# A new written-out order for the same 2,997 steps: DeltaNet attention and an MLP block

## The chip, the cores and the metric

The kernel runs on one core of a Trainium2 chip. The metric is the time of one execution on the device, in microseconds (us). TensorE is called PE here, VectorE DVE, ScalarE ACT, GpSimd POOL and the queue of SyncE SP.

## What is computed

Everything is fp32. The reference runs a DeltaNet recurrence over q, k, v of shape (4, 8, 768, 48), that is 4 batches, 8 heads, 768 tokens, head size 48:

```
state = 0                                       # per batch and head, 48 x 48
for t in range(768):
    kt = k[t] / (norm(k[t]) + 1e-6)
    y[t]  = q[t] @ state
    state = state + beta[t] * outer(kt, v[t] - state^T kt)
```

The heads are then laid side by side (x has 384 columns), and an MLP with a layer norm follows:

```
xn  = (x - mean(x)) / sqrt(var(x) + 1e-6) * g_ln
out = x + relu(xn @ w_ch1) @ w_ch2              # 384 -> 1536 -> 384
```

## The kernel before

The 768 tokens are cut into 12 chunks of 64. For a chunk the recurrence becomes matrix products plus the inverse of a unit lower triangular 64x64 matrix for each of the 32 (batch, head) pairs.

- **Start, chunk 0.** `first_inverse` builds that inverse by doubling, in five levels n = 1..5, for two groups g of heads. A level is a product E_n (PE, L722), a copy of E_n under a mask (DVE, L731), a product Z_n (PE, L741), transposes back (DVE, L687) and copies into the inverse `xt` (ACT, L681). Ahead of it stand the transposed keys (`first_kt`, PE L568, ACT L573), the products of keys with keys (`first_g`, PE L635), the key sums and norms (`first_norms`, ACT L594, DVE L595 to L602) and the first scaled G: `gsb <- product * ndb`, DVE L695. The masks are made on DVE from two iotas of POOL: six masks, each of three steps "ma" (L395), "mb" (L402) and "mask" (L408). POOL also copies an identity into seven buffers (L421).
- **Chunks 1 to 11.** `rows_inverse` solves 32 rows for two chunks at a time on DVE (62 small multiply and subtract steps, L860 and L867), `join` (PE L898 and L904, with a DVE transpose L888 ahead) doubles 32 to 64, and `recur` carries the state (PE L983, L1017, L1024, L1034). Results go through DRAM between these stages: `gd` (G), `xd` and `xt` (the inverse), `xld` and `xnt` (normed rows).
- **MLP.** Chunk 0 is done by halves (L1326, L1341). Chunks 1 to 3 multiply by w_ch1 directly (L1300), later chunks with a scheme of fifteen products (`fifteen`, L1221, with DVE L1241); the second product uses a scheme of seven (`seven`, L1423, with sums and differences of `h_all` on POOL, L1410, and outputs on DVE, L1441).

Nothing of this runs in the order in which the code states it. `add()` only notes a step with its engine and what it reads and writes; a step is one instruction of DVE, ACT, POOL or SP, or one group of matmuls on PE. A string `ORDER` then lists all 2,997 step numbers, and `emit()` issues them in that order:

```
for n in stated_order():
    if n < 0:
        self.filler()
        continue
    fn, deps = self.steps[n]
    assert deps <= out and n not in out
    fn()
```

Each engine works through its own steps strictly in the order of the list, waiting where an operand is not ready. DMA starts are steps of the queue that issues them: most are SP's, the loads of weights are ACT's, some loads of keys and beta POOL's. The entry `z` in the list issues the filler, a matmul of an identity with a broadcast column (128x128 by 256 columns, two passes, L1515), whose result nobody reads.

The steps that the prediction speaks of by number: 12 `eye`; 14, 17, 20, 23, 26, 29 the "ma" steps of masks 0 to 5; 82 and 89 the key sums; 110 the first scaled G; 122 and 124 E_1 of the two groups; 126 and 132 Z_1; 355 the first `u` product (L1000); 200 Z_5 of group 1; 359 the first half of the output of chunk 0 (L1024); 339 G of chunk 2 (L775); 577 the DVE transpose ahead of `join(3)`; 578 its first product; 941 a product of L1423.

Of the kernel before, what the change touches and what calls it, by code (L numbers as in the profile page):

```python
# [59 lines left out]
1 9 49 50 8 63 52 51 10 5 250 54 71 11 56 0 6 14 7 12 47 62 53 48 23 13 72 55 36 18 64 42 26 37 61 27 58 60 77 81 15 28 17 32 331 43 73 88 29 40 65 79  # L60
24 19 82 68 78 21 89 74 95 16 76 20 90 75 98 83 80 84 22 85 34 91 86 96 87 33 25 92 97 93 4 35 30 94 110 99 100 111 101 112 114 66 116 122 113 211 210
117 102 70 208 123 115 103 118 233 126 104 124 69 127 105 107 128 119 31 121 106 125 120 252 129 223 132 38 221 138 108 134 39 139 109 222 251 140 135
204 131 130 234 136 3 674 144 137 67 57 133 213 254 146 224 141 149 2 209 413 235 44 142 147 45 253 244 212 143 256 145 150 255 242 205 41 154 153 416
155 243 148 238 151 236 332 152 225 675 156 z 215 157 240 159 158 214 237 239 160 216 162 161 257 46 241 168 164 166 333 206 165 334 245 207 417 163
419 169 174 170 343 258 226 175 172 259 173 415 171 176 381 177 425 260 227 261 167 178 344 217 228 180 179 248 414 263 345 335 386 346 219 182 262
677 186 264 181 420 183 265 266 192 267 268 189 246 336 269 270 218 193 229 220 188 185 184 187 59 271 196 422 190 272 191 231 273 426 194 274 197 199
275 198 421 338 276 247 355 382 277 195 249 384 356 337 359 278 678 279 679 280 200 230 281 361 232 363 387 339 282 364 201 383 391 283 202 203 385
389 373 357 284 375 388 376 374 396 285 590 390 340 358 341 588 591 286 681 342 401 379 287 392 288 289 594 394 290 953 291 347 589 595 292 348 380
293 360 393 350 598 294 362 395 592 368 599 349 442 295 680 441 406 296 351 427 369 815 593 444 297 814 428 443 298 676 602 424 299 352 687 596 300
603 353 301 445 302 399 303 304 377 597 612 305 817 306 606 354 307 418 308 613 607 309 365 423 600 310 397 311 614 689 312 601 366 313 610 314 816  # L70
315 615 611 316 409 604 317 819 318 319 616 818 605 320 404 321 617 322:324 407 608 398 483 325 378 400 402 326 367 629 487 609 370 481 403 371 618
630 480 429 372 446 627 486 485 619 682 628 405 482 633 484 631 329 634 408 330 447 632 410 327 328 448 449 956 479 821 635 820 411 637 809 620 810
638 488 636 621 489:491 641 492 494 622 639 430 493 691 623 495 640 690 496 642 431 497 686 498 624 499 500 822 643 435 434 693 645 501 433 962 502
688 432 503 644 651 957 1100 504 505 436 692 506 507 652 438 508 439 509 647 440 510 437 811 653 511 512 964 450 666 1102 513 654 514 1099 451 515 655
516 517 454 518 965 519 966 1104 520 656 961 455 521 951 456 452 522 463 958 457 646 458 657 453 1215 464 649 465 807 523 459 658 808 524 466 460 1105
525 659 963 467 461 1106 694 950 468 683 462 955 526 660 1112 527 684 1101 528 469 1111 529 473 648 650 695 530 475 474 531 470 476 532 471 661 472
696 533 857 534 1114 535 697 536 967 855 537 858 1213 538 539 685 662 540 856 541 823 542:545 825 546:548 861 663 549:551 863 552 862 553:556 667 867
557 864 968 668 665 869 824 879 868 702 880 959 664 960 859 1214 669 873 860 560 1272 559 672 1103 865 561 812 670 558 705 826 477 866 699 874 698 870
701 888 969 412 706 871 703 885 700 875 704 671 872 1216 566 881 889 625 876 877 895 563 1217 813 567 878 1222 890 564 569 915 882 570 827 562 891 568
886 898 571 565 916 707 1107 896 626 899 572 1115 1212 900 708 883 576 892 709 574 884 901 573 1224 710 1116 893 575 902 954 887 894 917 903 1380 1113  # L80
828 904 1221 1558 711 713 905 829 923 918 577 712 897 924 832 714 715 673 925 716 833 717 906 718 834 926 719 912 835 907 841 836 927 1274 842 919 928
837 1560 908 838 929 920 843 913 839 909 844 941 840 720 910 721 830 845 921 914 846 847 722 922 1377 851 723 578 1264 1223 849 930 724 1557 1226 579
942 725 580 1562 831 931 1218 852 943 850 1118 853 932 848 726 581 1117 933 854 727 582 944 911 728 934 945 729 935 730 970 936 1227 731 938 1376 583
732 937 971 1225 972 585 1273 1228 584 587 1210 1563 733 946 734 1006 952 735 939 736 737 1004 738 974 973 947 1005 739 1007 586 1028 1010 740 1029
1119 1564 1559 975 1229 1011 1031 1008 1561 741 1385 742 1570 940 743 1569 1012 744 1009 745 746 1016 747 1013 976 748 749 1014 1387 750 1017 1572
1386 751 478 1211 979 752 1571 1015 1378 753 754 977 980 755 981 756 1018 1389 757 988 982 989 1384 1573 978 990 1379 1020 983 758:760 1022 761 1021
762 991 984 763 1390 1019 764 1108 985 765 949 1023 1034 1391 766 1230 986 767 948 1109 768 769 1388 1037 770 987 771 1110 1026 772 773 992 774 775
993 994 1038 776 1027 1024 995 1670 1044 1231 996 1030 1120 1265 1025 1275 1047 1035 1121 1039 1064 1040 1048 1122 1045 780 1041 1032 777 1049 1033
778 1065 1042 1036 779 1050 1043 1066 1126 1046 1051 1000 1054 1219 1266 1233 998 1268 997 1232 1276 999 1267 1127 1052 1055 1131 1053 1067 1565 1128
1061 1056 1072 1124 1270 1068 1125 1073 1392 1220 1069 1129 1074 1002 1057 1130 1001 1070 1075 785 1003 784 1058 1269 1076 781 1234 1079 1277 782 1059  # L90
1080 1271 783 1060 1077 1081 1680 2035 1078 786 1373 1062 1090 787 1123 1082 790 1091 789 1083 788 1063 1278 1092 2037 1279 1084 1682 1132 1071 1093
1681 1085 791 1302 1133 1086 1280 793 1134 792 1135 794 1136 1138 795 1094 1284 1137 2039 1139 1140 1235 1141 1285 1142 1281 1143 796 1305 1095 1303
1236 1668 1290 2034 1096 1684 1144 1087 1374 1145 2041 1282 1146 1291 1673 2036 1147 1148 1574 1088 1149 1237 1150 1283 1669 1151 1152 1239 1098 1153
1154 797 1155 1156 1296 1157 799 800 1158 1241 1686 1159 1288 1576 1160 1297 1304 1248 1161 2040 1311 1162 1289 1286 1238 1249 1250 1163 1381 1294
1164 1858 1287 1382 1165 1240 1383 1679 801 1312 1675 1295 1292 1251 1089 1166 1167 1685 1313 1168 1293 1674 1393 1252 1242 1169 798 1253 1855 1308
1243 1395 1375 1309 1244 1857 1306 1245 802 1318 1397 1097 1314 1300 1394 1319 1307 1298 1170 1575 1301 1171 803 805 1172 1246 1321 1173 1315 1247
1174 1322 1299 1255 1316 804 1310 806 1323 1254 1317 1396 1175 1256 1320 1683 1176 2038 1398 1672 1177 1178 1324 1179 1399 1338 1180 1325 1676 1181
1339 1326 1340 1327 1328 1182 1341 1260 1346 1183 1342 1184 1257 1347 1185 1343 1186 1259 1348 1344 1329 1687 1258 1349 1335 1353 1330 1350 1187 1354
1863 1188 1331 1189 1853 1351 1190 1402 1336 1191 1263 1345 1352 1261 1400 1262 1192 1404 1193 1194 1355 1865 1411 1195 1332 1412 1196 1356 1197 1413
1364 1198 1333 1414 1365 1334 1337 1450 1199 1441 1366 1200 1401 1440 1451 1455 1201 1427 1403 2150 1577 1357 1405 1430 1406 1367 1851 1358 1457 1439  # L100
1566 1852 1415 1431 1456 1359 1416 1429 1407 1688 1443 1408 1859 1567 1432 1409 1418 1368 1444 1202 1452 1410 1435 1203 1369 1433 1204 1454 1458 1370
1205 2047 1453 1417 1208 1460 1434 1459 1419 1361 1862 1464 1442 1461 1568 1436 1462 1866 1466 1437 1671 1467 1463 1867 1438 1578 1465 1360 1445 1690
1362 1446 1469 1468 1579 1447 1689 1422 1428 1471 1448 1470 1449 1474 2049 1472 1477 1581 1584 1475 1473 1580 1480 1860 1423 1861 1478 1363 1483 1479
1481 1583 1476 1691 1421 1484 2051 1489 1420 1694 1486 1485 1582 1693 1490 1692 1487 1502 1496 1588 1491 1503 1587 1488 1677 1492 1678 1504 1695 1585
1493 1206 1505 1494 1586 1506 1497 1495 1371 1701 1426 1516 1869 1589 1498 1696 1703 1868 1507 1499 1699 1529 1207 1424 2042 1509 1697 1517 1372 1744
# [1547 lines left out]
```

## Time and profile before

| | |
|---|---|
| time, median of 3 runs | 510.0 us (508.62 to 510.16) |
| the profiled execution | 510.58 us, of which its span is 508.8 us |
| mean granted PE clock | 0.965 |
| PE busy | 488.6 us (96%), 9606 matmul passes |
| DVE busy | 353.8 us (70%) |
| ACT busy | 249.0 us (49%) |
| POOL busy | 275.6 us (54%) |
| chain that ended last | PE 90%, DVE 5%, issue 2%, POOL 1%, DMA 1% |

A busy time is a sum over the instructions of an engine. The clock is the share of full speed that PE was granted. In the chain that ended last every step is followed back to what released it, so 90% of PE says that over most of the span the end waits for PE alone.

### The profile page before, as it was taken

The page shows a single profiled execution, that of the slowest core. Times are in us where ns is not written, and L with a number is a line of the kernel's source. Part 1 is how long each engine was busy: PE and PEld are TensorE (multiplying, and loading weights), DVE is VectorE, ACT ScalarE, POOL GpSimd, SP SyncE. Part 2 cuts the span into 40 slices and gives each one's busy share as a digit, 9 for nine tenths or more (in the row PEclk, how much of TensorE's full clock was granted, in tenths as well). Part 3 has the DMA queues.
Part 4 walks back from the last instruction along what each step waited for, and adds up shares of the span by engine and source line. Part 5 has one row for each costly group of instructions (what it writes and reads, how often), then busy time and mean ns, then how long its engine had stood idle before and what let it go on. Part 6 is the DMA issues. An engine that isn't in the chain of part 4 may idle for free.

```text
span 508.8 us, 22190 instructions
## 1 busy us (share of the span) xinstructions
PE 488.6 (96%) x9606; PEld 447.6 (88%) x9606; DVE 353.8 (70%) x780; ACT 249.0 (49%) x620; POOL 275.6 (54%) x430
## 2 busy tenths in 40 slices
PE   7778999999899999999999999999999999999996
PEld 3667988788788898899999999999999999999996
DVE  9668987997679648896649898568899328143251
ACT  5758873643544524627435535435563257363230
POOL 5464537264755496438894363492543850645633
PEclk9756799999999999999999999999999999999999
DMA  8988796667656566546834434766154402211101
GB/s 168 293 160 190 249 200 85 98 152 130 90 86 87 187 119 119 65 99 149 194 58 62 94 62 135 150 94 97 50 92 106 111 20 45 60 48 46 24 18 31
DMA packets 196097, 54.99 MB, mean 108 GB/s; under 512 B 186076, under 2 KB 189404, under 8 KB 196000
## 3 DMA queue, kind: packets, MB, share of 16 engines
q1 hardware_dynamic: 189920, 40.58, 41.9%
q10 hardware_dynamic: 3872, 9.83, 6.0%
q0 software_dynamic: 2208, 3.17, 3.8%
q8 instruction: 75, 1.23, 1.0%
q14 instruction: 22, 0.18, 0.1%
HBM read 36.64 MB, written 16.91 MB: 105 GB/s over the span
## 4 chain that ended last, share of the span: by engine, by line
PE 90%; DVE 5%; issue 2%; POOL 1%; DMA 1%; SPq 0%; ACT 0%; DVEq 0%; POOLq 0%; ACTq 0%
PE f L1423 29%; PE f L1221 22%; PE f L1300 9%; PE f L1326 4%; PE f L1341 3%; PE by L983 2%; PE by L1024 2%; PE two L983 2%; PE by L775 2%; PE two L1017 2%; PE two L775 2%; PE two L1034 2%; PE f L775 1%; DMA xt<-xd 1%; PE by L741 1%
## 5 line engine op out<-in xcount | busy, mean ns | idle before, releaser
L1410 POOL TENSOR_TENSOR h_all<-h_all 128x256 f32<-128x256 f32 x123 | 89.9, 742 | 135.1 <-PE f L1423 121.3
L1423 PE MATMUL f<-w_sb,h_all 128*128 128x192 f32 x492 | 109.8, 332 | 1.6 <-DVE rstd L967 1.6
L1423 PEld LDWEIGHTS f<-w_sb,h_all 128*128 128x128 f32 x492 | 81.8, 190 | 3.6 <-issue 1.9
L1423 PE MATMUL f<-words,h_all 128*128 128x192 f32 x396 | 84.5, 330 | 0.3 <-POOL h_all L1410 0.3
L860 DVE TENSOR_TENSOR tmp<-xb,gb 128x87 f32<-128x87 f32 (+21 forms) x186 | 73.7, 396 | 4.9
L867 DVE TENSOR_TENSOR xb<-xb,tmp 128x87 f32<-128x87 f32 (+21 forms) x186 | 73.6, 396 | 4.8
L1241 DVE TENSOR_TENSOR h_all<-h_all,f 128x512 f32<-128x512 f32 x96 | 63.5, 682 | 14.3 <-PE f L1221 13.2
L1423 PEld LDWEIGHTS f<-words,h_all 128*128 128x128 f32 x396 | 66.6, 190 | 1.7 <-POOL h_all L1410 1.0
L1300 PE MATMUL f<-xnt,w_sb 128*128 128x256 f32 x216 | 50.2, 382 | 0.0
L349 POOL DMA_DIRECT2D tb<-in_k_dram x64 | 42.0, 660 | 10.3 <-DVE kt L755 9.4
L1243 ACT ACTIVATE h_all<-h_all 128x512 f32<-128x512 f32 x48 | 28.5, 624 | 34.6 <-DVE h_all L1241 34.3
L1300 PEld LDWEIGHTS f<-xnt,w_sb 128*128 128x128 f32 x216 | 40.2, 190 | 5.3
L1237 ACT COPY h_all<-f 128x512 f32<-128x512 f32 x48 | 26.2, 590 | 34.3 <-PE f L1221 17.4
L1441 DVE TENSOR_TENSOR o<-f,x 128x192 f32<-128x192 f32 x33 | 11.6, 352 | 38.9 <-PE f L1423 22.3
L1221 PE MATMUL f<-words,w_sb 128*128 128x128 f32 x256 | 31.7, 276 | 0.0
L1309 ACT ACTIVATE h_all<-f 128x256 f32<-128x256 f32 x36 | 13.3, 382 | 35.1 <-PE f L1300 34.9
L1221 PEld LDWEIGHTS f<-words,w_sb 128*128 128x128 f32 x256 | 30.0, 192 | 0.2
L1221 PE MATMUL f<-xnt,w_sb 128*128 128x128 f32 x192 | 25.4, 276 | 0.0
L542 POOL TENSOR_TENSOR w_sb<-words 128x768 uint32<-128x768 uint32 (+1 forms) x11 | 15.0, 1365 | 17.7 <-DVE words L529 13.3
L1221 PEld LDWEIGHTS f<-xnt,w_sb 128*128 128x128 f32 x192 | 23.7, 192 | 0.1
L1326 PEld LDWEIGHTS f<-xnt,w_sb 128*128 128x128 f32 x144 | 19.2, 200 | 3.3 <-issue 0.2
L1088 ACT ACTIVATE xnt<-xnt,g_sb 128x256 f32<-128x256 f32 x27 | 12.5, 498 | 19.2 <-DMA xnt<-xld 19.1
(246 smaller groups left out, 958.4 us busy)
## 6 DMA issues: line engine op xcount, KB each, us to landing
words<-in_moe_w_ch_dram ACTq DMA_DIRECT2D x10, 768.0 KB, 5.2
gd<-gsb SPq DMA_DIRECT2D x11, 512.0 KB, 3.6
v<-in_v_dram SPq DMA_DIRECT2D x24, 192.0 KB, 4.3
kr<-in_k_dram SPq DMA_DIRECT2D x46, 96.0 KB, 3.6
out_dram<-o SPq DMA_DIRECT2D x44, 96.0 KB, 2.8
xld<-xlt SPq DMA_DIRECT2D x9, 384.0 KB, 3.3
xnt<-xld SPq DMA_DIRECT2D x36, 96.0 KB, 3.2
gb<-gd SPq DMA_DIRECT2D x44, 64.0 KB, 3.0
```

The source lines that it names most:

```text
L349: add(eng, cost, lambda: QUEUE[eng].dma_start(out=out_, in_=in_), r, w, bulk=n * ns / 16e3, **kw)
L775: nc.tensor.matmul(pair[hp][half(e ^ (hp & n)), (g * NP + j) * C : (g * NP + j + 1) * C], kt[drows(hp), l], rt[drows(hp), i],)
L860: lambda j=j, n=n, w=w, t=t: nc.vector.tensor_tensor(out=t, in0=xv[:, 0:n, j : j + 1].to_broadcast([np_, n, w]), in1=gv[:, j : j + 1, j + ...
L867: "DVE", dve(n * w), lambda t=t, rest=rest: nc.vector.tensor_tensor(out=rest, in0=rest, in1=t, op=ALU.subtract),
L1221: nc.tensor.matmul(wide(p[:, 128 * n : 128 * n + 128]), w[n // 2][:, n % 2 * 128 : n % 2 * 128 + 128], r, start=start and n == 0, stop=Tru ...
L1237: add("ACT", act(512), lambda: nc.scalar.copy(o, p), pk, ok)
L1241: add("DVE", dve(512), lambda: nc.vector.tensor_tensor(out=o, in0=o, in1=p, op=op), pk, ok)
L1243: add("ACT", act(512), lambda: nc.scalar.activation(o, o, ACTF.Relu), [], ok)
L1300: nc.tensor.matmul(p[:, 0:TOK], w1_sb[:, t, f * 128 : (f + 1) * 128], xnt[:, t], start=(t == 0), stop=(t == KC - 1))
L1326: nc.tensor.matmul(p[:, 0:128], w1_sb[:, t, f * 128 : (f + 1) * 128], xnt[:, t, cols], start=(t == 0), stop=(t == KC - 1))
L1410: add(eng, cost, lambda: e.tensor_tensor(out=out_, in0=x, in1=y, op=op), r, w, port=2 if eng == "Pool" else 1, pr=-2)
L1423: lambda f=f, t=start and f == 0: nc.tensor.matmul(p[:, 0:D2], lhs(f), rhs[:, f], start=t, stop=(f == F2 - 1), skip_group_check=True),
```

## The change

Only the string `ORDER` changes; all its 93 lines are new. The set of step numbers is the same, every step still comes after those that it depends on, and `z` occurs three times instead of once. The first lines of the diff, cut:

```
 ORDER = """
-1 9 49 50 8 63 52 51 10 5 250 54 71 11 56 0 6 14 7 12 47 62 53 48 23 13 72 55 36 18 64 42 26 37 61 27 58 60 77 81 15 28 17 32 331 43 73 88 29 40 65 79
-24 19 82 68 78 21 89 74 95 16 76 20 90 75 98 83 80 84 22 85 34 91 86 96 87 33 25 92 97 93 4 35 30 94 110 99 100 111 101 112 114 66 116 122 113 211 210
...
+62 5 52 49 47 71 50 63 51 48 8 54 9 6 10 1 7 53 0 57 11 72 56 251 55 12 4 60 14 32 42 61 250 74 76 331 77 81 40 88 78 65 82 34 73 58 79 64 41 83 68 95
+17 36 89 33 97 13 37 90 80 98 29 30 15 3 84 75 100 96 23 85 31 86 91 99 16 87 27 110 210 35 101 18 66 111 102 92 112 113 115 93 103 94 122 26 28 70 19
...
```

Read engine by engine, it does this:

| engine | before | after |
|---|---|---|
| DVE, ahead of step 110 | 38 steps: all "ma" and "mb", masks 0 to 4, the norms of both groups | 28 steps: only masks 0 and 5 are made, the norms of group 1 (92 to 94) follow later |
| DVE, between 110 and the copy of E_1 of group 1 (125) | 9 steps, among them mask 5 | 20 steps, among them masks 1 to 4 |
| POOL, first steps | iotas, beta, a 0.97 us memset, identity matrix, then copies | two loads of beta, iotas, identity matrix, another load of beta, then memsets and copies mixed |
| PE, first level | 122, 102, 126, 124, 107, 106, 132, 138 | 102, 122, 126, 106, 107, 124, 138, 132, z |
| PE, fourth level | 177 (E_4 of group 1), 180 (Z_4 of group 0), 335, 186, 192 | 180, 177, 186, 335, 192 |
| PE, the filler | once, ahead of E_3 of group 1 | once ahead of step 204 (a product of queries and keys), once between 355 and 200, once between 359 and 339 |
| PE, after 355 | 359, 200, 339 | z, 200, 359, z, 339 |
| DVE, near `join(3)` | 577 ahead of the sums 929 and 921 and of 839 and 845 (layer norm of chunk 2) | 577 behind them |
| SP | transfers spread between each other in one way | 386 transfers in another order; two thirds of them change their place |

Of PE's 816 steps 501 keep their order among each other (the longest common subsequence), of DVE's 780 steps 565, of ACT's 589 steps 317, of POOL's 426 steps 206, of SP's 386 steps 127.

## The prediction

> **What bounds it now.** Read first: the busy table and the 40 slices on the page.
>
> ```profile
> span 508.8 us, 22190 instructions
> PE 488.6 (96%) x9606; PEld 447.6 (88%) x9606; DVE 353.8 (70%) x780; ACT 249.0 (49%) x620; POOL 275.6 (54%) x430
> PE   7778999999899999999999999999999999999996
> PEclk9756799999999999999999999999999999999999
> ```
>
> PE is full in all slices (12.7 us each) but the first four and the last, and its clock is below full only in the first five. The chain that ended last agrees: 90% PE, 5% DVE, 2% issue. So a new order can gain in three places only: PE's idle time, its clock, the passes it is given. Its idle time, from the waits of PE and PE's timeline:
>
> ```profile
> PE f L775 <- issue: 2.5, 2, 1.6
> PE f L1423 <- DVE rstd L967: 1.6, 1, 1.6
> PE by L741 <- issue: 1.5, 1, 1.5
> ```
>
> Columns: who waits for whom, us in total, times, longest. PE idles 15.9 us ahead of its end at 504.6; 13.0 of them lie before 50 us, and 2.9 after, of which 1.60 is one gap at 138.25 and 0.81 a stall at 143.02. The "issue" stalls lie where PE's count of weight loads and matmuls reaches 449, 705, 961, 1217, exactly 256 apart, and queue q8 (instruction) has 75 packets of 16 KB: code is being fetched. They hang on the count, which a new order keeps (each filler adds four).
>
> The clock, from the windows view, columns as named in its head: PE, PEld, DVE, ACT and POOL busy, granted clock, DMA share, GB/s:
>
> ```profile
> 18.90:22.31 3.41, 3.41 (x65) 3.08 (x68) 1.21 (x4) 2.46 (x5) 2.95 (x4) 0.50 0.99 391
> 46.20:49.62 3.42, 2.70 (x76) 2.44 (x72) 3.21 (x9) 3.30 (x7) 2.17 (x3) 0.50 0.90 85
> 49.62:53.03 3.41, 3.41 (x107) 3.22 (x99) 3.34 (x8) 3.10 (x8) 1.91 (x3) 0.50 0.54 96
> 53.03:56.44 3.41, 3.38 (x43) 2.96 (x42) 3.41 (x5) 2.31 (x7) 2.55 (x3) 0.50 0.77 246
> 56.44:59.86 3.42, 3.42 (x91) 3.08 (x93) 3.18 (x9) 2.80 (x6) 0.53 (x1) 1.00 1.03 404
> ```
>
> The clock changes on a grid of 3.41 us; from 15.48 it is half to 56.44, apart from 22.31 to 25.72 and 42.79 to 46.20, and full from there on. Each full stretch followed a half one that was busy for 3.38 or 3.41 and held 1.1 to 2.0 us of 128x128 passes (by the same view of one line: L568 1.97 in 18.90 to 22.31 and 1.11 in 39.38 to 42.79, L1326 1.98 in 53.03 to 56.44). One condition alone was not enough: 49.62 to 53.03 was busy throughout, but with 64-row products, and half clock followed; 29.14 to 32.55 held the filler (1.22) but was busy for 3.05 only, and half clock followed.
>
> **The change, part by part.** All sums are made against the profiled execution, 510.58 us (508.8 span and 1.8 around it). The median, 510.0, lies 0.58 below it; about 0.3% (1.5 us) is what a measurement of this kernel can tell from no change.
>
> *a. The start, to step 355 (begins 46.37).* Up to 110 (begins 11.14) DVE is the bound, and the timeline shows why it is late:
>
> ```profile
> 4.19 0.62 POOL L421 COPY gsb<-u 128x512 f32<-128x512 f32 x1
> 4.74 0.62 POOL L421 COPY pt<-u 128x512 f32<-128x512 f32 x1
> 5.30 0.61 POOL L421 COPY gsb<-u 128x512 f32<-128x512 f32 x1
> 3.80 2.38 DVE L402 TENSOR_SCALAR xb<-xb 128x64 int32<-128x64 int32 x1
> 6.09 1.06 DVE L402 TENSOR_SCALAR xb<-u 128x64 int32<-128x64 int32 x1
> 8.10 0.54 DVE L595 TENSOR_REDUCE ksum<-xln 128x8 f32<-128x384 f32 x1
> ```
>
> Start, duration, instruction. An L402 step takes 0.18 undisturbed; this one took 2.38, until three copies of POOL back to back were over, the next 1.06 beside two more. Key sum 82 had its operand from ACT at 6.63 and ran at 8.10. The new order takes 10 steps net from ahead of 110 (mask steps of 0.18 to 0.22, starts some 0.1 apart: 1.1 us) and may let 82 run near 6.7. Against it: POOL issues two loads of beta (0.72 and 0.52) ahead of the iotas that all masks start from, so these come 1.2 later; its copies now follow load 57, two memsets of 0.97 between them, and so start near 4.9 and last past 8.5; and the steps open to starvation (14, 17, 29, 30, 15, all TENSOR_SCALARs) now stand before and between the two key sums, so that a stall of 1.06 to 2.38 is passed on to 110. Without any stall 110 comes 0.9 earlier (sums at 6.7 and 7.6, then the seven small steps to 110 as before); with one stall of 1.06 to 2.38 it comes 0.2 to 1.5 later. I take +0.8, since copies back to back did this both times they met an L402. [...]
>
> From 110 on the five levels are one chain of PE, DVE and ACT. Each edit there: E_1 of group 0 before L568's last passes, the masks between 110 and 125 (nine steps more, of about 0.1 to 0.2 at their starts; cover: DVE waits for PE in this stretch, 1.2 busy of 3.41 in the window at 18.90), and the filler ahead of 204: at nothing, the 1.60 code stall at 22.97 hides them (the price without it 1.15 for the filler). The filler ahead of E_3 of group 1 goes: -1.15 (row L1515 at 30.98), but the code stall behind it (34.67, 1.53) begins later in count and takes back about half: -0.5. Z_4 of group 0 ahead of E_4 of group 1: nothing to +0.4, since PE waits 0.99 at 37.70 for DVE's copies and the swap asks for the other one first; I take +0.35, as that wait is the nearest row. DVE's transposes 187 and 188 ahead of copy 193: +0.35. With 0.8 from above: 0.8 - 0.5 + 0.35 + 0.35 = **+1.0** at step 355, bounds -0.7 (no starvation) and +1.6 (a second one).
>
> *b. The fillers behind 355 and 359.* Two of 1.15 at half clock are 2.30; PE idled 0.65 at 48.02, waiting for the DVE copy ahead of 359, and step 200 now stands there too: 2.30 - 0.65 = **+1.65**; at full clock half of it less the same gap, +0.5. Nothing else covers them: PE has no other idle time from 48.67 to 63.
>
> *c. The clock.* The fillers are 128x128 passes, and with 355 ending near 49 they start at about 49 and 52: at least one, 1.15 us, lies in 49.62 to 53.03, which was busy already. By the pattern above that window is followed by full clock: from 53.03 instead of 56.44. 3.41 us at half clock are 1.7 of full work: **-1.7**; one window earlier it would be -3.4, no change 0. I take the middle value: the window that ends at 49.62 gets a part of one filler at most. [...]
>
> *d. The steady state.* The gap at 138.25:
>
> ```profile
> 135.79 0.71 DVE L888 STREAM_TRANSPOSE xnj<-xt 128x512 f32<-128x512 f32 x1 [2.63 <-DMA xt<-xd]
> 139.35 0.35 DVE L1441 TENSOR_TENSOR o<-f,x 128x192 f32<-128x192 f32 x1
> ```
>
> DVE's queue is in order: 577 waited 2.63 for a transfer of 5.08 us, and the sums behind it (929, 921), which free the PSUM that L1423 wants, came late. Now they stand ahead of 577, and those behind 577 have no such hurry: -1.6. Elsewhere room moves both ways. I counted PE's work between the last issue of the transfers and the first product of each of eleven joins: six have more or the same, five less; the least of these are e4, from 9.2 to 6.6 us, and e6, from 10.0 to 6.3. Their need is the 5.08 of the row plus 0.71 for the transpose, 5.8, so they still fit by 0.5 to 0.8. SP now reaches 20 transfers (before: 5) less than 3 us after one that they depend on, 3 us being the page's usual landing; each can hold SP's later issues. I allow +0.4, bounds 0 and +4. Sum **-1.2**. The tail is in nearly the same order: 0.
>
> **Sum.** +1.0 + 1.65 - 1.7 - 1.2 = -0.25, so 510.3 on the profiled execution, **509.7** against the median. The range of this case alone: 508.6 to 511.4.
>
> **Rivals.**
> 1. *Full clock by 49.62.* The window from 46.20 grows dense (its 0.72 of idle filled by a filler) and the rate doubles at once: c is -3.4, fillers +1.65: sum -1.95, **508.0**. For it: that 1.11 of wide passes was enough at 39.38; against it: with 355 later, less than one filler fits there. [...] Chance .22.
> 2. *A fast start.* POOL's copies miss the L402s or yield: a is -0.7, sum -1.95, **508.1**. Against it: both stalls of 2.38 and 1.06. Chance .11.
> 3. *Paid fillers without the clock* (the other side). 355 begins 1.6 later, so the fillers straddle 49.62 and neither window holds enough; half clock to 56.44: +1.6 + 1.65 + 0 - 1.2 = +2.05, **512.0**. It decides if no full-rate window begins before 56.4. For it: the dense window at 49.62 and the filler at 30.98, which brought nothing. Chance .22.
> 4. *SP held back* (slower too). A transfer waited for in SP's queue delays those of e4 or e6 by over 0.8 us, the point from which PE waits; two or three gaps like that at 138.25 (1.6 each): d is +2 instead of -1.2, sum +2.95, **513**. For it: 20 against 5 tight starts. Against it: after 50 us PE waited for a transfer, through DVE, only at 138.25. Chance .15.
> The change not doing what it says is the same as a's middle value: masks moved, but starvation takes the room.
>
> **How the numbers follow.** The forecast has .30, and its range lies within 1.5 us of 510. Rivals 1 and 2 (.33) make "faster", 3 and 4 (.37) "slower". The likeliest time is 509.7. Down, the range takes in both fast rivals at once (-0.7 + 1.65 - 3.4 - 1.2 = -3.65, 506.4, put at 506.5); up, rival 4 with 0.5 more, 513.5.
>
> **What would show it.** Right: 110 later than 11.14 and an L402 of over 1 us near POOL's copies; 355 near 47.4; granted clock 1.00 from 53.0; the wait of L1423 for rstd L967 gone; PE's end near 504.3. Wrong: 110 before 10.5; full clock at another place; PE waits of over 0.5 us after 60 us on L898 or L1423, behind a DMA; a code stall off the counts named.

## The result and the profile after

| | before | after |
|---|---|---|
| median of 21 executions each, in turn on the same chips | 508.19 us (506.35 to 511.52) | 510.53 us (509.08 to 516.78) |
| ratio, 95% interval | 1 | 1.0048 (1.0028 to 1.0067) |
| mean over more executions (standard error) | 508.46 us (0.12), the 148 that stand beside the experiments | 510.35 us (0.28), 20 of these 21 and 12 later ones |
| the profiled execution, its span | 510.58, 508.8 us | 510.01, 508.1 us |

The new order is slower by 0.48% over the first 21 executions and by 1.9 us (0.37%) over all. One execution of after, at 516.78, was in a slower state and is left out of the ratio and of the mean. Executions of one and the same program differ by 0.6 to 2.0 us (standard deviation over its executions), and the profiled execution of before was a late one: 2.1 us above the mean of its kernel. The profiled execution of after lies 0.3 below the mean of its own. So the two spans, 508.8 and 508.1, tell the wrong way round, and no single pair of profiles shows where 1.9 us went. What follows rests on events that come again in several traces, and on means over executions.

The page after, the lines that answer to those of before:

```profile
span 508.1 us, 22179 instructions
PE 489.8 (96%) x9610; PEld 448.0 (88%) x9610; DVE 347.1 (68%) x780; ACT 247.5 (49%) x620; POOL 275.9 (54%) x430
PE   8679999998999999999999999999999999999996
PEclk9955899999999999999999999999999999999999
```

The four more passes are the two added fillers. Next, the waits of PE from 60 us on (who waits for whom, us in total, times, longest):

```profile
PE f L898 <- DVE xnj L888: 1.4, 1, 1.4
PE f L898 <- issue: 0.6, 1, 0.6
PE by L1096 <- ACT xln L969: 0.5, 1, 0.5
PE f L1341 <- issue: 0.5, 1, 0.5
PE f L1423 <- ACT words L1455: 0.3, 1, 0.3
```

The wait of L1423 for rstd (1.6) is gone, as forecast, and two new ones stand in its place: step 567, a product of join 2 (L898), and step 469 (L1096).

The start on DVE, from the timeline (start, duration, instruction, idle time before it):

```profile
4.13 1.01 DVE L395 TENSOR_SCALAR xb<-u 128x64 int32<-128x64 int32 x1
6.90 0.55 DVE L595 TENSOR_REDUCE ksum<-xln 128x8 f32<-128x384 f32 x1 [0.88 <-ACT xln L594]
8.96 0.64 DVE L402 TENSOR_SCALAR xb<-xb 128x64 int32<-128x64 int32 x1
10.82 0.69 DVE L695 TENSOR_TENSOR gsb<-two,ndb 128x512 f32<-128x512 f32 x1
```

The first key sum runs at 6.90 (8.10 before), the longest L402 takes 0.64 (2.38 before), and the first scaled G begins at 10.82 instead of 11.14. Mask steps are still longer beside POOL: step 14 (L395) took 1.01, beside a memset of POOL (L1540, 4.09 to 5.05), where such a step takes 0.18 elsewhere in the start, but ahead of the key sum, and DVE then waited 0.88 for ACT all the same.

The clock behind step 355, in windows (PE, PEld, DVE, ACT, POOL busy, granted clock, DMA share, GB/s):

```profile
44.01:47.42 3.41, 2.43 (x34) 1.56 (x34) 2.13 (x7) 3.10 (x6) 2.09 (x2) 0.50 0.85 120
47.42:50.83 3.41, 3.41 (x79) 2.67 (x82) 2.86 (x8) 1.39 (x7) 0.89 (x1) 0.50 0.93 269
50.83:54.25 3.42, 3.42 (x99) 2.88 (x92) 1.81 (x5) 2.73 (x7) 1.76 (x2) 0.50 0.18 40
54.25:57.66 3.41, 3.41 (x87) 3.23 (x84) 3.05 (x7) 2.26 (x6) 2.41 (x3) 1.00 0.72 158
```

Full clock from 54.25, about where it was forecast. But the fillers ran at 46.27 and 49.31; the window that holds the second, busy throughout, was followed by half clock, and the one that was followed by full clock holds none.

### The profile page after: what moved, and what is told of

The parts are those of the page before. It is cut to its first block, busy times and chain, and to the rows that moved or that the text cites. A ratio compares the mean times of both kernels' runs of the same rounds, so it can differ in the third digit from the quotient of the medians.

```text
span 508.1 us, 22179 instructions
## 1 busy us (share of the span) xinstructions
PE 489.8 (96%) x9610; PEld 448.0 (88%) x9610; DVE 347.1 (68%) x780; ACT 247.5 (49%) x620; POOL 275.9 (54%) x430
## 4 chain that ended last, share of the span: by engine, by line
PE 81%; DVE 9%; DMA 3%; issue 2%; SPq 2%; ACT 1%; POOL 0%; DVEq 0%; ACTq 0%; POOLq 0%
PE f L1423 30%; PE f L1221 22%; PE f L1300 6%; DVE tmp L860 3%; DVE xb L867 3%; PE by L1024 2%; SPq L349 2%; PE by L983 2%; PE by L775 2%; PE two L983 2%; PE two L1017 2%; PE two L1034 2%; DMA xt<-xd 1%; PE two L775 1%; PE by L741 1%
## 5 line engine op out<-in xcount | busy, mean ns | idle before, releaser
L1423 PE MATMUL f<-w_sb,h_all 128*128 128x192 f32 x492 | 108.5, 330 | 0.3 <-ACT words L1455 0.3
L1423 PE MATMUL f<-words,h_all 128*128 128x192 f32 x396 | 85.0, 330 | 0.0
L1423 PEld LDWEIGHTS f<-w_sb,h_all 128*128 128x128 f32 x492 | 82.5, 190 | 2.3 <-ACT words L1455 0.6
L867 DVE TENSOR_TENSOR xb<-xb,tmp 128x87 f32<-128x87 f32 (+21 forms) x186 | 74.0, 398 | 4.8
L860 DVE TENSOR_TENSOR tmp<-xb,gb 128x87 f32<-128x87 f32 (+21 forms) x186 | 72.9, 392 | 5.0
L1423 PEld LDWEIGHTS f<-words,h_all 128*128 128x128 f32 x396 | 66.5, 190 | 1.4 <-POOL h_all L1410 0.6
L1221 PE MATMUL f<-words,w_sb 128*128 128x128 f32 x256 | 32.5, 277 | 0.0
L542 POOL TENSOR_TENSOR w_sb<-words 128x768 uint32<-128x768 uint32 (+1 forms) x11 | 15.0, 1371 | 22.5 <-DVE words L529 14.0
L1062 ACT ACTIVATE x<-by 128x384 f32<-128x384 f32 x23 | 11.1, 484 | 27.2 <-PE by L1024 21.7
## 6 DMA issues: line engine op xcount, KB each, us to landing
gd<-gsb SPq DMA_DIRECT2D x11, 512.0 KB, 4.7
```

The source lines that it names most:

```text
L860: lambda j=j, n=n, w=w, t=t: nc.vector.tensor_tensor(out=t, in0=xv[:, 0:n, j : j + 1].to_broadcast([np_, n, w]), in1=gv[:, j : j + 1, j + ...
L867: "DVE", dve(n * w), lambda t=t, rest=rest: nc.vector.tensor_tensor(out=rest, in0=rest, in1=t, op=ALU.subtract),
L1221: nc.tensor.matmul(wide(p[:, 128 * n : 128 * n + 128]), w[n // 2][:, n % 2 * 128 : n % 2 * 128 + 128], r, start=start and n == 0, stop=Tru ...
L1423: lambda f=f, t=start and f == 0: nc.tensor.matmul(p[:, 0:D2], lhs(f), rhs[:, f], start=t, stop=(f == F2 - 1), skip_group_check=True),
```

## The experiments

The kernels were run in groups, in turn with the kernel before on one chip; a ratio is taken to the executions of before in the same group, 12 executions a kernel unless said otherwise. Half-clock time is 2 x span x (1 - mean granted clock), averaged over the executions; the clock granted in the traces of before and after is 0.50 or 1.00 throughout. A change of the list is shown as the entries of one engine.

### Is it the start or the rest?

`start_after` takes the new order up to step 379 of PE (56.91 before) and the old one behind it, `start_before` the reverse; both kernels were also run again unchanged.

> The kernel before, unchanged, for a second profile. Both theories: ratio 1.000. It separates what is fixed by the order from what changes between executions. If the time lost by the new order is lost in the start (theory S), PE's idle time after 60 us here is within 0.5 us of the new order's 3.0 us; if it is lost behind the start (theory R), it is lower here by 1.5 to 2.5 us, the gap of 1.60 at 138.25 among what is gone.

> The new order, unchanged, for a second profile. Both theories: ratio 1.003 to 1.007. Theory R: the gaps of PE at 125.17 (1.44 us, ahead of L898), 71.71 (0.54) and 102.26 (0.54) come again. Theory S: they are gone or differ, and the steps 355 and 379 begin no earlier than in the kernel before.

> The new order up to step 379 of PE (its three fillers with it), the order before behind it. Theory S (the two late fillers cost 2.3 us, and the clock would have risen as early without them): ratio 1.003 to 1.006. Theory R (the rest of the order costs it): 0.998 to 1.001.

> The order before up to step 379 of PE (one filler), the new order behind it. Theory S: ratio 0.998 to 1.001. Theory R: 1.003 to 1.006, with PE gaps ahead of L898, L1341 and L1096 as in the new order.

| kernel | ratio (95%) | half-clock us | 355 to 379 | 379 to the end of row solve 2 | wait of 469 | wait of 567 |
|---|---|---|---|---|---|---|
| before_again | 0.9999 (0.998 to 1.0018) | 32.6 | 10.1 | 58.9 | 0 | 0.20 |
| after_again | 1.0016 (0.9987 to 1.0044) | 35.0 | 14.5 | 60.8 | 0.54 | 0 |
| start_after | 1.0018 (1.0001 to 1.0035) | 35.0 | 13.0 | 58.5 | 0 | 0 |
| start_before | 1.0015 (0.9995 to 1.0034) | 32.5 | 11.4 | 61.2 | 0.54 | 0.44 |

The last four columns are from the one trace of each, except the half-clock time. Neither theory holds alone: `start_after` is 0.8 us over before and `start_before` 0.75 (standard error 0.4 each), so each part gives something like half of the 1.9. That is the mean over groups; `after_again` itself came out at 1.0016, under the 1.003 to 1.007 that was expected and no more than either part. (In `before_again` PE idles 1.8 us behind 60 us, in the first trace of before 2.9: the gap of 1.60 didn't come again.) With the rest of the new order come the wait of 469 and a row solve that ends 2 to 3 us later (62.0 in the first trace of after, 58.4 in that of before). With the new start come the longer stretch from 355 to 379 and some 3 us more at half clock.

The rest, read in the trace of after. On ACT the copy 684 (L796) now stands ahead of 462 (the second L969), which step 469 of PE waits for:

```profile
100.73 0.60 ACT L969 ACTIVATE xln<-xln,rstd 128x384 f32<-128x384 f32 x1
101.24 0.99 ACT L796 COPY gsb<-two 128x1024 f32<-128x1024 f32 x1
102.13 0.61 ACT L969 ACTIVATE xln<-xln,rstd 128x384 f32<-128x384 f32 x1
```

PE was free at 102.26 and ran 469 at 102.80. And in the second half of row solve 2, DVE first, then POOL:

```profile
109.64 2.33 DVE L860 TENSOR_TENSOR tmp<-xb,gb 128x156 f32<-128x156 f32 x1
113.03 0.27 DVE L860 TENSOR_TENSOR tmp<-xb,gb 128x112 f32<-128x112 f32 x1
113.33 1.43 DVE L867 TENSOR_TENSOR xb<-xb,tmp 128x112 f32<-128x112 f32 x1
114.80 1.41 DVE L860 TENSOR_TENSOR tmp<-xb,gb 128x87 f32<-128x87 f32 x1
116.24 0.39 DVE L867 TENSOR_TENSOR xb<-xb,tmp 128x87 f32<-128x87 f32 x1
110.65 0.45 POOL L1449 TENSOR_TENSOR words<-h_all 128x128 f32<-128x128 f32 x1
111.06 0.72 POOL L1167 TENSOR_TENSOR qt<-w_sb 128x256 f32<-128x256 f32 x1
113.03 3.06 POOL L622 TENSOR_TENSOR v<-v,knrm 128x768 f32<-128x768 f32 x2
```

The same two DVE steps in the trace of `before_again`:

```profile
110.40 0.73 DVE L860 TENSOR_TENSOR tmp<-xb,gb 128x156 f32<-128x156 f32 x1
112.89 0.28 DVE L867 TENSOR_TENSOR xb<-xb,tmp 128x112 f32<-128x112 f32 x1
```

Two products of POOL of 1.5 us each (steps 960 and 813) lie beside the solve; the DVE step that meets one takes 1.43 and 1.41 where it takes 0.28 and 0.25, and ends 0.1 to 0.2 behind the product (114.76 and 116.21 against 114.6 and 116.09). A third step, 545 (L860 at 109.64), takes 2.33 beside four short POOL steps back to back, two of L1449 and two of L1167 (109.55 to 111.78); it takes 0.73 or less in all eleven traces with the old order there, and 2.32 or 2.33 in all eight with the new one. The old order has a collision too: 960 stands beside step 544, which takes 1.50. The solve ends at 117.76; its result goes through two transfers to the transpose 566 (125.84), and 567 waits 1.44.

### The two places put back, and put into the old order

```
ACT   684 462                          ->  462 684
POOL  812 ... 1115 960 813 881 ... 895 ->  812 960 ... 1115 881 ... 895 813
```

`rest_repaired` is `start_before` with this edit. `before_spoiled` is the kernel before with the reverse (684 ahead of 462, and 960 and 813 behind 477, beside the end of the solve; 8 executions).

> The kernel start_before with three steps put back to where the order before has them: on ACT the normed rows 462 ahead of the copy 684 (0.99 us), on POOL the products 960 and 813 (v times a norm, 1.5 us each) away from the last steps of the second row solve on DVE. Theory P (these two places are what the rest of the new order loses): PE's gap of 0.54 ahead of step 469 is gone, the row solve ends some 58.5 us after 379 begins (61.0 in the new order, 58.3 before), the gap ahead of 567 is under 0.2, and the ratio is 0.999 to 1.0005 instead of 1.0015. Rival Q (a general loss by the order of SP's transfers): both gaps gone, but others take their place and the ratio stays at 1.001 to 1.002.

> The kernel before with the two places of the new order that rest_repaired put back: POOL's products 960 and 813 beside the last steps of the second row solve, ACT's copy 684 ahead of 462. Theory P: the row solve's last steps take 1.4 us beside them and it ends some 61 us after 379 begins (58.3 before), PE waits 0.5 ahead of step 469 and 0.4 to 1.5 ahead of 567; ratio 1.0015 to 1.003. Rival Q: ratio 1.000 to 1.001.

`rest_repaired`: 1.0000 (0.9975 to 1.0025), 0.8 us less than `start_before` by the ratios, with a standard error of 0.7, so the time alone doesn't show the repair. `before_spoiled`: 1.005 (1.0029 to 1.0072), the whole loss of the new order and more. The wait of 469 goes and comes with the edit: it is absent from the list of PE's waits of `rest_repaired`, and in that of `before_spoiled`:

```profile
PE f L1423 <- DVE rstd L967: 1.6, 1, 1.6
PE f L898 <- issue: 0.9, 1, 0.9
PE by L1096 <- ACT xln L969: 0.8, 1, 0.8
```

The row solve answers less well. In `rest_repaired` it still ends 60.2 behind 379 (58.5 was expected): the edit left the largest collision, 545 at 2.32 beside L1449 and L1167 (`after_repaired`, below, keeps it without a loss of time), and 960 now costs one step 1.50, as in the old order. 567 still waits 0.45. In `before_spoiled` two steps take 1.40 and 1.41, but 960 has left its old place, so that the 1.50 there is saved; the solve ends at 59.1 and 567 waits 0.14 only. So the collision is shown, step by step; what it costs PE is 0 to 1.4 us from one execution to the next, and the 1.84 us (standard error 0.4) of `before_spoiled` are more than its trace accounts for.

### The fillers

```
PE   355 359 200 339    ->  355 z 359 z 200 339   (before_fillers)
PE   355 359 200 339    ->  355 z z z 359 200 339 (before_burst, 8 executions)
PE   355 z 200 359 z    ->  355 200 359           (after_one_filler, start_after_plain)
```

> The kernel before with a filler behind 355 and one behind 359, nothing else. Theory F: 1.0 to 2.0 us more, ratio 1.002 to 1.004. Theory C: 0.997 to 1.001, with full clock one window earlier.

> The kernel start_after without the two fillers behind 355 and 359. Theory F (the two fillers are 2.4 us of PE time for nothing but an idle 0.65, and don't bring the full clock forward): 1.0 to 2.0 us less than start_after's 1.0018, so a ratio of 0.998 to 1.000, and 379 begins some 11 us after 355, not 13. Theory C (the fillers pay by an earlier full clock): 1.002 or more, with the full clock one window of 3.41 us later.

> The new order without its two late fillers, nothing else. If the fillers cost what before_fillers showed (0.8 us): ratio 1.002 to 1.003, against 1.0035 for the new order over its 32 runs so far. If they cost nothing here: 1.003 to 1.004. If they cost 2 us: 0.999 to 1.000.

> The kernel before with three fillers back to back behind 355 (instead of one there and one behind 359). Theory W, read from the ten traces so far: what decides the clock is the sum of active rows x active columns x moved columns over a window of 3.41 us; above some 23.5 million full clock follows, below it half, and a single filler (8.4 million in 1.22 us, 6.9 a microsecond) only equals the mean that is needed. Three in a row give 25.2 million in some 2.9 us, 8.6 a microsecond: at least one window passes, and full clock begins between 50 and 54 instead of 55 to 59. Cost 2.9 less 0.65 of idle, gain about 2.4: ratio 0.998 to 1.002. Rival B (busy time alone decides, or chance): full clock at 55 or later, and ratio 1.004 or more.

| kernel | ratio (95%) | half-clock us | 355 to 379 | full clock from |
|---|---|---|---|---|
| before_fillers | 1.0013 (0.9991 to 1.0036) | 32.2 | 12.3 | 56.7 |
| start_after_plain | 1.0022 (0.9994 to 1.005) | 35.4 | 11.3 | 56.2 |
| after_one_filler | 1.0029 (1.0006 to 1.0051) | 36.4 | 11.2 | 55.6 |
| before_burst | 1.0062 (1.0037 to 1.0087) | 28.4 | 9.7 | 42.8 |

The clock gains nothing by the two fillers: half-clock time is 32.2 with them and 32.5 without in the old start, and 36.0 with and 35.9 without in the new one (means of 44 and 36 executions). They cost time: 0.8 us in the old order (standard error 0.4); between `after` and `after_one_filler` some 0.7 by their distances to before; between `start_after` and `start_after_plain` nothing that can be told, where 1 to 2 us were expected. The mean of the three, weighted by their errors, is 0.6 us (0.3).

Why they don't pull the clock up is read from the windows. I summed for each window of 3.41 us, over its matmuls, active rows x active columns x moved columns. In the traces of before and after, 15 windows at half clock with 10.6 to 20.9 million were followed by half clock and four with 23.5 to 27.9 million by full clock. In 19 traces there are 179 such windows ahead of 66 us: split at 23.4 million, 173 are followed by full clock above and by half clock below. Some 23.5 million were read from the first ten traces; of the 84 windows of the nine later ones a split there tells 81. Being busy says less: of 67 windows that were busy for 3.38 us or more, 37 were followed by full clock. (Of 140 windows at full clock a split at 21.3 million tells 138 and one at 21.9 tells 139.) 23.4 million in 3.41 us are 6.9 a microsecond, and that is what the filler gives (8.4 million in 1.22 us). The products behind 355 give 3.9 (L741), 5.7 (L1000, L1024) or 6.4 (L775) where they lie close; one filler and 2.2 us of these make 22.5 million at most, so by this estimate a filler among them leaves a window below 23.4 million. The windows of after behind 44 us have 14.2, 20.9 and 23.5 million, and only the third is followed by full clock.

`before_burst` was to show this: 25 million in a row. Its half-clock time is the least of all kernels (28.4, standard error 1.3, against 30.9 of before in that group and 32.5 over all groups), which speaks for an earlier full clock. But its time is 2.5 us longer, 1.0062 where 0.998 to 1.002 was expected. Its trace can't show the step itself, as the clock was full from 42.78. It shows something else: a gap of PE of 1.83 at 138.72 was followed by two windows at half clock. The window that holds it has 21.6 million; those that hold the gaps of 1.57 to 1.74 in three other traces have 23.0 to 24.6, and the clock stayed.

```profile
138.36:141.77 3.41, 1.58 (x41) 1.09 (x42) 3.27 (x11) 2.08 (x6) 1.29 (x3) 1.00 0.31 34
141.77:145.19 3.42, 3.42 (x119) 2.93 (x108) 3.32 (x8) 0.39 (x2) 3.42 (x6) 0.50 0.22 36
145.19:148.60 3.41, 3.41 (x11) 3.41 (x12) 0.78 (x3) 3.21 (x10) 1.14 (x2) 0.50 0.89 140
```

### Why the new start has more half clock

Slid over the traces of the kernels with the old start, a window that begins in some 2.6 of the 3.41 us about 38 passes 23.4 million; it holds step 335 (L568, 128x128 passes) among Z_4 and E_4. With the new start and 335 behind 186 such windows begin in 0.6 us at most.

```
PE   180 177 186 335 192  ->  180 177 335 186 192  (after_335, after_repaired_335)
PE   177 180 335 186 192  ->  177 180 186 335 192  (before_335_late)
```

`after_repaired` is the new order without the late fillers and with the three steps of ACT and POOL put back; `after_repaired_335` has 335 put back as well.

> The new order without its two late fillers and with the same three steps put back. Theories F and P: the whole loss is gone, ratio 0.996 to 0.9995. If only one of them holds: 1.001 to 1.003. If neither: 1.003 to 1.006.

> The new order with one PE step put back: 335 (L568, passes of 128x128) ahead of 186 (a Z_4), as before; fillers and all else as in the new order. Theory K (this move costs the full-clock window near 42): slid over the trace, windows that start in some 2 us about 38 reach 23.6 million again; over 12 executions the half-clock time, 2 x span x (1 - mean clock), is 32 to 34 us instead of 35.9; 0.8 to 1.5 us less time: ratio 1.001 to 1.0025. Rival: half-clock time stays at 35 to 37, ratio 1.003 to 1.004.

> The kernel before with 335 behind 186, nothing else. Theory K: the stretch of windows over 23.6 million about 38 is gone, half-clock time 35 to 36 us instead of 32.5, ratio 1.001 to 1.003. Rival: half-clock time 32 to 33 and ratio 0.999 to 1.001.

> after_repaired with 335 ahead of 186: the new order's start and its place of 577, without the two late fillers, the three steps of the rest and 335 put back. Theory K: half-clock time 32 to 34 us instead of 35.7, ratio 0.996 to 0.999, so less than both kernels. Rival: 0.9995 to 1.001.

| kernel | ratio (95%) | half-clock us (standard error) |
|---|---|---|
| after_repaired | 1.0002 (0.9974 to 1.003) | 35.7 (0.7) |
| after_335 | 1.0037 (1.0017 to 1.0056) | 36.1 (1.2) |
| before_335_late | 0.999 (0.9962 to 1.0017) | 35.5 (1.1) |
| after_repaired_335 | 0.9996 (0.9974 to 1.0019) | 34.5 (1.2) |

`after_repaired` speaks for fillers and collisions as the loss: without them the new order runs like the old. Its own interval leaves room for 1.5 us, but with `after_repaired_335` it is 0.3 us (0.3) below before, against 1.9 above for the new order. The theory on 335 falls: moved late in the old order it shows 35.5 us at half clock, against 33.7 (0.9) of before in that group, and no loss of time; and in its trace the dense windows about 38 still begin in 2.7 us, so the move didn't undo them. Put back in the new order it brings neither clock nor time. So why the new start has more half clock stays open in the main, and that half clock there costs so little fits PE's many waits ahead of 355 (13.0 us of idle time before 50 us in the first trace of before), if a faster clock only makes them longer; that was not tried.

### The gap at 138

```
DVE  577 714 ... 929 839 720 721 845 921  ->  714 ... 929 839 720 721 845 921 577
```

`before_577` has this edit alone, `before_577_plain` leaves out the one filler as well.

> The kernel before with the transpose 577 behind 929, 839, 845 and 921 on DVE, as in the new order. Part d of the prediction: PE's gap of 1.6 to 1.7 at 138 (seen in two of five traces that have the old order there) is gone; worth 0.3 to 0.9 us on the mean of many runs, ratio 0.998 to 0.9995. Rival: the gap comes back ahead of 578, ratio 1.000.

> before_577 once more, beside the last: part d of the prediction says 0.3 to 0.9 us less than before, ratio 0.998 to 0.9995; no gap of 1.6 us near 138.

> before_577 without the one filler that the order before has (ahead of E_3 of group 1). If fillers cost their PE time and bring no clock (theory F): 0.3 to 1.0 us less than before_577, ratio 0.996 to 0.9985, less than both kernels. If that filler is hidden by the code stall behind it, or keeps the clock up: 0.999 to 1.001.

0.9992 (0.9972 to 1.0012) and again 0.9995 (0.9975 to 1.0016): 0.4 us less (0.3). The gap of 1.6 to 1.8 stands in four of eight traces that have 577 ahead of the sums (the old order with or without other edits), and in none of eleven that have it behind. In that of `before_577_plain`:

```profile
136.81 0.36 DVE L1441 TENSOR_TENSOR o<-f,words 128x192 f32<-128x192 f32 x1
137.08 0.70 DVE L888 STREAM_TRANSPOSE xnj<-xt 128x512 f32<-128x512 f32 x1
```

577 begins without a wait, behind the sums. `before_577_plain` is the best version of all: 507.04 us median, 0.9974 (0.9956 to 0.9993), less than both kernels. Beside `before_577_again` in the same group it has 0.9 us less (0.4): the filler ahead of E_3 was not worth its time either.

## Why the prediction was wrong

The forecast was 0.3 us less, and it is 1.9 more; the time lies inside the range, the sign is the other.

- **The base.** All terms were put on one profiled execution, 2.1 us above the mean, and the median of three was 1.5 above it. The gap at 138.25 is part of that: a late transfer that half of the traces have.
- **a, the start (+1.0 at 355).** The stall came, but what it would delay was wrong. It fell on steps 12 and 14 (1.36 and 1.01) ahead of the key sums, where DVE then waited for ACT; 82 ran at 6.90, near the 6.7 of the case without a stall. The prediction put 29, 30 and 15 before and between the sums, but in the list they stand behind both; there they took some 0.6 instead of 0.18 each (no L402 over 0.65 in any trace with the new start), and 110 came 0.3 to 0.4 earlier, not 0.8 later and not 0.9 earlier. At 355 the traces show no difference: it begins at 45.3 on the mean of eight with the new start and at 45.5 on that of eleven with the old one. All of the new start but the fillers is worth 0 to +1.0 us (`after_repaired`, `start_after_plain`).
- **b, the fillers (+1.65).** In the traces 355 to 379 takes 12.9 with the two fillers and 10.9 without (four traces each, new start): the size was right there. In the time 0.6 (0.3) of it is left; a later 379 gives the row solve time that it lacks otherwise (`after_again`: 379 at 61.7 and no wait of 567).
- **c, the clock (-1.7).** This step is enough to turn the sign: with 0 in its place the prediction's own sum is +1.45. That a busy window with 1.1 us of 128x128 passes is followed by full clock was read from three windows; the sum of work, split at 23.4 million, tells 173 of 179 windows, and the two windows of after that hold the fillers have 14.2 and 20.9 million. Measured: 0 (32.2 us at half clock with the fillers and 32.5 without, 36.0 and 35.9 with the new start).
- **d, the steady state (-1.2).** The gap went, as forecast, but is worth 0.4 instead of 1.6, as it was there in half of the executions only. The allowance of +0.4 was the larger miss: the copy ahead of 462 and the new collisions, some 1.2 (`start_before` with the 0.4 of the gap added) to 1.8 us (`before_spoiled`). With the +0.8 of `start_before` in place of -1.2 the sum is again above zero. I had counted SP's order and the room behind transfers from places in the list, without the row solve, which DVE ended 2 to 3 us later beside POOL's steps: of the DVE steps beside POOL I had looked at the L402 steps alone. The new order of SP was not tried alone; `after_repaired` and `after_repaired_335` keep it and lose nothing that can be measured.

Of the rivals, the third came nearest in kind (512.0): fillers paid and no clock for them, though not for its reason, fillers that straddle a boundary, and in the first trace of after not by its sign either, as full clock came at 54.25 and not behind 56.4. The fourth named waits at the joins, but not their cause. Together 0.6 (fillers), 0.8 to 1.0 (the rest, net of the gap) and some 0.3 (the start) give the 1.9 within their errors.

## What to carry to other kernels

When a static order is changed, list for each long chain of DVE steps which POOL instructions now stand beside it, by time and not by place in the list: here the steps of the row solve that took 1.4 to 2.3 us (L867 at 113.33, L860 at 114.80 and at 109.64) ended 0.1 to 0.2 behind the last POOL step that they met, 1.2 to 1.6 us later than otherwise. Before a gap of one trace is counted as a gain, see in two or three more traces whether it comes every time. Two fillers of 6.9 million a microsecond, the mean of a window of 23.4 million, bought no clock here (half-clock time 32.2 us with them and 32.5 without); count rows x columns x moved columns for the window (173 of 179 windows told) rather than busy time (37 of 67 busy windows followed by full clock).

## What was not expected of the hardware

- The sum of work (rows x columns x moved columns) in a window of 3.41 us went with the clock of the next one: in 19 traces a split at 23.4 million tells 173 of 179 windows at half clock, and one at 21.3 or 21.9 million 138 or 139 of 140 at full clock.
- One gap of 1.83 us in the steady state was followed by 6.8 us at half clock; gaps of 1.57 to 1.74 at the same place were not.
- The time around the span is the same for all executions of a program, within 0.07 us of their mean, but not for all programs: 1.72 before, 1.90 after, 2.16 for `start_after`, 2.01 for `after_repaired`, 1.71 to 1.75 for all kernels with the old start. So 0.2 of the 1.9 us lie outside the span. With the old start it is the same whatever follows, with the new one it is not; what it is, no run here shows.
- Code stalls at one and the same pass (347, L775) last 1.49 us in the trace of after, 1.60 in that of before and 4.1 in that of `start_before`, so that they alone can make two executions differ by more than the 1.9 us of the change.
